# Scaling the first chunk's tokens behind the projection, spreading beta by a product, and a new order on all engines, in a one-core transformer block

## The chip, the core and the metric

The kernel runs on one core of one Trainium2 chip. The metric is the time of one execution on the device, in microseconds, taken as the median of several timed runs. Beside the timed runs there is one profiled execution with its own time; its trace records what each engine did: TensorE (PE, with its weight loads PEld), VectorE (DVE), ScalarE (ACT), GpSimd (POOL), SyncE (SP, which here issues transfers) and the DMA queues. Times within the trace count from its first instruction.

## The reference

One pre-layernorm block on 2048 tokens of width 576, all in bfloat16: an attention with a memory, and a feed-forward part.

```python
def _layernorm(x, axis=-1, eps=1e-05):
    m = jnp.mean(x, axis=axis, keepdims=True)
    v = jnp.var(x, axis=axis, keepdims=True)
    return (x - m) / jnp.sqrt(v + eps)

def _A_ref(x, wq, wk, wv, wo, beta):         # H = 32 heads of 18, N = 4 segments of L = 512 tokens
    q, k, v = x @ wq, x @ wk, x @ wv         # cut into heads and segments
    g = _sigmoid(beta).reshape(1, H, 1, 1)
    for s in range(N):
        p = softmax(q[s] @ k[s].T * 18 ** -0.5 + causal mask)
        a_dot = p @ v[s]
        a_mem = phi(q[s]) @ M / (phi(q[s]) @ z + 1e-06)
        o[s] = g * a_mem + (1.0 - g) * a_dot
        M, z = M + phi(k[s]).T @ v[s], z + phi(k[s]).sum(tokens)
    return o @ wo                            # phi(t) = t + 1 where t > 0, exp(t) elsewhere

def _B_ref(x, w1, b1, w2, b2):               # F = 4608
    return _gelu(x @ w1 + b1) @ w2 + b2

h = x + _A_ref(_layernorm(x), ...)
out = h + _B_ref(_layernorm(h), ...)
```

## The kernel before

The 2048 tokens are worked in 8 chunks of 256, each of two tiles of 128 tokens; two chunks make a segment. The work on TensorE is written as streams (Python generators) that are woven into each other:

- `stream_P(tl)`, one for each of a chunk's two tiles: load x, layernorm, transpose the normalised tile (on TensorE in the first two chunks, by a transposing DMA later), project it to q, k and v. A projection is five products (`mm5`, lines 607 to 610: four on 128 rows of the width, one on the last 64 with a row of zeros). In the first chunk it is cut into six groups of 288 columns, later into four of 432. Each group's bank of PSUM is evicted to bfloat16 by `move` (lines 687 to 689), a plain copy on ScalarE or VectorE.
- `stream_A`: scores of a query tile against key tiles (`scores`, line 817, four heads at once on 32 rows of the array each), one exponential over all four score banks (line 823, 128x2048), the causal mask on GpSimd or VectorE (lines 828 and 830), the weighted sum (line 849 or 862) and its division (`finish`). There is one set of score banks.
- `stream_M`: the memory matrices; `stream_B(tl)`: the product with wo, the residual, the second layernorm.
- `stream_F1` and `stream_F2`: the feed-forward part. F1 takes w1 in 9 column groups per chunk (`load_w1`, streamed again for every chunk into a ring of buffers), with products on 128 rows (line 1167) and on 64-row halves (line 1154), adds b1 in the eviction (line 1175 or 1177) and applies the gelu on ScalarE (line 1189). F2 (line 1223) multiplies by w2, which stays on the chip.

The **layernorm** (lines 612 to 635) is statistics on VectorE (line 617, two halves), their aggregation and the addition of epsilon (lines 621 and 622), a power of -0.5 on GpSimd (line 627), and then one VectorE instruction that subtracts the mean and multiplies by the power (line 631). For the first chunk all of it stands ahead of the first product.

**Beta** is loaded by a GpSimd DMA into all 128 partitions (line 571); `gates` makes the sigmoid and its complement of it on ScalarE and VectorE.

**What sets the order.** While the program is built, the function first simulates itself with a list of estimated durations and due times (`op`, `begin`, `step`, `SLACK`, `PHASES`); this makes a list of operations. What is sent to the engines is something else: `arranged` (line 1313) goes through the written list `ORDER` of operation numbers, found by a search, and issues each in that order; a negative number means that the operation runs on its second engine (VectorE in place of ScalarE, say). `PLACE` gives the PSUM bank of each use. Every engine runs its instructions strictly in this order and waits on semaphores where it must, so a late operation holds up all that stand behind it on its engine. That includes SP, which issues nearly all transfers from one queue, and may have eight under way. At the start, where TensorE has nothing to do, products of zeros are put in (line 1295).

The products use four shapes of the array: 128x128, 64x128 (line 1154), 32x128 (scores) and 128x32 (weighted sums of later chunks).

## Time and profile before

| | |
|---|---|
| timed runs | 461.86, 466.97, 467.87 us (median 466.97) |
| profiled execution | 460.12 us, of which the trace's span is 458.4 |
| granted TensorE clock | 1.00 |
| PE busy | 449.2 us, 98% of the span, 6078 products |
| ACT busy | 318.9 us, 70% |
| DVE busy | 291.9 us, 64% |
| POOL busy | 152.4 us, 33% |
| DMA | 83.40 MB, 182 GB/s on average |

A busy time is the union of an engine's instructions. Products are pipelined: one starts before the one ahead of it has ended, so the mean time of a product is longer than the step between two starts, and a short stall can hide in the busy time. "Idle before" in a row is what the engine waited for just ahead of this instruction, with the releaser that came last.

### The profile page before, as it was taken

To read this page: it belongs to the slowest core of one execution; us is meant where nothing else is said; L and a number is where in the kernel's file an instruction comes from. 1 tells how busy PE (TensorE), PEld (TensorE's weight loads), DVE (VectorE), ACT (ScalarE), POOL (GpSimd) and SP (SyncE) were. 2 spreads that over 40 slices of the span, in tenths; PEclk is the share of its full clock that TensorE was granted. 3 is DMA by queue.
4 is the path that set the end of the run, shared out by engine and by line. 5 is a ranking of instruction groups with operands and counts; after the bars stand their busy time and mean duration, and the time that the engine had idled before them with its cause. 6 is when DMAs were issued, how large, how long until landed. Compare 5 with 4: busy or idle time off the path is not lost.

```text
span 458.4 us, 14431 instructions
## 1 busy us (share of the span) xinstructions
PE 449.2 (98%) x6078; PEld 333.8 (73%) x6078; DVE 291.9 (64%) x765; ACT 318.9 (70%) x309; POOL 152.4 (33%) x208
## 2 busy tenths in 40 slices
PE   7999999999999999999999999999999999999997
PEld 5778676676777777666677777677777888888874
DVE  6888888777788667778774757686564535212311
ACT  5888889887987958896565986788757954260420
POOL 5667254482345025573241312521222101000000
PEclk9999999999999999999999999999999999999999
DMA  7998978798997679799878787568966867574001
GB/s 217 312 308 163 262 191 159 166 220 176 180 183 200 197 207 215 136 187 200 160 172 165 209 214 169 141 166 166 248 194 188 189 189 228 160 222 137 28 14 39
DMA packets 137521, 83.40 MB, mean 182 GB/s; under 512 B 72800, under 2 KB 135664, under 8 KB 137456
## 3 DMA queue, kind: packets, MB, share of 16 engines
q1 hardware_dynamic: 137424, 82.47, 73.8%
q8 instruction: 47, 0.77, 0.7%
q14 instruction: 18, 0.15, 0.1%
q0 software_dynamic: 32, 0.01, 0.0%
HBM read 59.44 MB, written 6.49 MB: 144 GB/s over the span
## 4 chain that ended last, share of the span: by engine, by line
PE 85%; DMA 6%; DVE 4%; ACT 1%; POOL 1%; SPq 1%; issue 1%; ACTq 0%; POOLq 0%; DVEq 0%
PE bank L1223 23%; PE bank L1167 18%; PE bank L609 11%; PE late L1223 6%; PE st L817 5%; PE late L1167 4%; PE ox L849 4%; PE bank L1154 3%; PE bank L610 3%; DMA o_col<-oT 2%; PE bank L1127 2%; DMA xT<-o_nat 1%; PE ox L1167 1%; DMA KT<-qk_pad 1%; DMA w1g<-in_B_w_dram 1%; ACT pt L823 1%
## 5 line engine op out<-in xcount | busy, mean ns | idle before, releaser
L823 ACT ACTIVATE pt<-st 128x2048 bf16<-128x2048 f32 x80 | 150.2, 1877 | 42.3 <-PE st L817 22.7
L1223 PE MATMUL bank<-w_sb,hT 128*128 128x288 bf16 (+1 forms) x900 | 132.2, 288 | 0.0
L1223 PEld LDWEIGHTS <-hT 128*128 128x128 bf16 x1152 | 109.1, 98 | 30.0 <-issue 1.5
L828 POOL TENSOR_SCALAR_AFFINE_SELECT pt<-pt 128x512 bf16<-128x512 bf16 x87 | 56.2, 661 | 99.8 <-ACT pt L823 99.7
L1167 PE MATMUL bank<-xn2T,w1g 128*128 128x256 bf16 x656 | 82.2, 273 | 0.3 <-DMA w1g<-in_B_w_dram 0.3
L1189 ACT ACTIVATE hT<-hT 128x1536 bf16<-128x1536 bf16 (+3 forms) x26 | 66.3, 2567 | 22.9 <-DVE hT L1177 22.8
L1167 PEld LDWEIGHTS <-w1g 128*128 128x128 bf16 x752 | 70.4, 98 | 15.8 <-issue 5.7
L1177 DVE TENSOR_TENSOR hT<-bank,b1T 128x512 bf16<-128x512 f32 x73 | 49.6, 687 | 47.0 <-PE bank L1167 46.8
L609 PE MATMUL bank<-wqkv,xT 128*128 128x432 bf16 (+1 forms) x268 | 57.2, 336 | 1.0 <-DVE hT L1177 0.5
L609 PEld LDWEIGHTS <-xT 128*128 128x128 bf16 x400 | 37.0, 97 | 21.6 <-issue 1.5
L1175 ACT ACTIVATE hT<-bank,b1T 128x256 bf16<-128x256 f32 x64 | 26.7, 474 | 23.9 <-PE bank L1167 23.4
L817 PE MATMUL st<-QT,KT 32*128 32x128 bf16 x1280 | 32.3, 217 | 0.4 <-DMA KT<-qk_pad 0.3
L1223 PE MATMUL late<-w_sb,hT 128*128 128x288 bf16 x216 | 32.2, 286 | 0.0
L1167 PEld LDWEIGHTS <-wqkv 128*128 128x128 bf16 x288 | 27.3, 98 | 5.2 <-issue 1.3
L817 PEld LDWEIGHTS <-KT 32*128 32x128 bf16 x1280 | 18.6, 92 | 16.2 <-issue 12.8
L1033 POOL TENSOR_TENSOR h_t<-h_t,b_bc 128x576 f32<-128x576 f32 x16 | 20.7, 1297 | 23.3 <-issue 16.6
L849 PE MATMUL ox<-pt,v_aug 128*32 128x128 bf16 x1184 | 25.9, 221 | 0.0
L830 DVE TENSOR_TENSOR pt<-pt,causal 128x512 bf16<-128x512 bf16 x41 | 19.4, 484 | 9.2 <-ACT pt L823 9.2
L849 PEld LDWEIGHTS <-v_aug 128*32 128x32 bf16 x1184 | 17.3, 96 | 7.6 <-issue 4.5
L610 PE MATMUL bank<-wqkv,xT 65*128 65x432 bf16 (+1 forms) x67 | 22.6, 338 | 0.0
L1227 DVE TENSOR_TENSOR ot<-bank,hc 128x288 bf16<-128x288 f32 x24 | 10.9, 456 | 16.8 <-PE bank L1223 10.5
L1177 DVE TENSOR_TENSOR hT<-late,b1T 128x512 bf16<-128x512 f32 x13 | 8.6, 686 | 19.6 <-PE late L1167 19.5
(148 smaller groups left out, 633.7 us busy)
## 6 DMA issues: line engine op xcount, KB each, us to landing
w1g<-in_B_w_dram SPq DMA_DIRECT2D x49, 512.0 KB, 4.7
wqkv<-in_B_w_dram SPq DMA_DIRECT2D x18, 512.0 KB, 4.8
w_sb<-in_B_w_dram SPq DMA_DIRECT2D x6, 864.0 KB, 8.2
hd<-h_t SPq DMA_DIRECT2D x14, 288.0 KB, 3.2
hc<-hd SPq DMA_DIRECT2D x28, 144.0 KB, 3.0
w1g<-in_B_w_dram SPq DMA_DIRECT2D x98, 32.0 KB, 3.2
x_b<-in_A_x_dram SPq DMA_DIRECT2D x18, 144.0 KB, 3.9
hT<-in_B_w_dram SPq DMA_DIRECT2D x5, 512.0 KB, 4.1
```

What stands on the lines that cost most here:

```text
L609: nc.tensor.matmul(out=out_ap, lhsT=lhsT_of(slice(0, P), k), rhs=rhs_of(slice(0, P), k), start=(k == 0), stop=False)
L610: nc.tensor.matmul(out=out_ap, lhsT=lhsT_of(slice(0, KTAIL), 4), rhs=rhs_of(slice(0, KTAIL), 4), start=False, stop=True)
L817: nc.tensor.matmul(out=st4[:, i, n * P:(n + 1) * P], lhsT=KTs[(c - c % 2 + kt // 2) % 3][rows, g, (kt % 2) * P:(kt % 2 + 1) * P], rhs=QTs[ ...
L823: op("ACT", 1.88, lambda: nc.scalar.activation(out=pt[:], in_=st4[:], func=ACT.Exp, scale=scale), sk, [("pt", slot, n) for n in range(4)], ...
L828: either(("POOL", 0.64, lambda part=part: nc.gpsimd.affine_select(out=part, in_=part, pattern=[[0, 4], [1, P]], compare_op=ALU.is_ge, fill ...
L849: nc.tensor.matmul(out=ox[32 * i:32 * i + 32, g % 4 * P:(g % 4 + 1) * P], lhsT=v_flat[(2 * s0 + kt) % 6][:, h * E:h * E + 32], rhs=pts[slo ...
L1033: op("POOL", 1.29, lambda: nc.gpsimd.tensor_tensor(out=h_t[:], in0=h_t[:], in1=b2_bc[:], op=ALU.add), ["b2"], [("h", tl)], slack=SLACK["hb"])
L1167: nc.tensor.matmul(out=bank(b)[:, a * Q:(a + 1) * Q], lhsT=w1_main(wt)[:, k, (2 * (h % 2) + a) * P:(2 * (h % 2) + a + 1) * P], rhs=xn2T[c ...
L1175: nc.scalar.activation(out=hT[:, f + a, :], in_=bank(b)[:, a * Q:(a + 1) * Q], func=ACT.Identity, bias=b1T[:, f + a:f + a + 1])
L1177: either(("DVE", 0.69, lambda hT=hT, f=f, b=b: nc.vector.tensor_tensor(out=hT[:, f:f + 2, :], in0=bank(b)[:].rearrange("p (a w) -> p a w", ...
L1189: op("ACT", (f1 - f0) * Q * 0.00083 + 0.18, lambda hT=hT, f0=f0, f1=f1: nc.scalar.activation(out=hT[:, f0:f1, :], in_=hT[:, f0:f1, :], fun ...
L1223: nc.tensor.matmul(out=acc, lhsT=hT[:, q, tl * P:(tl + 1) * P], rhs=w2_sb[:, q, hs], start=(q == 0), stop=(q == NF - 1))
```

## The change

It has these parts.

1. In the first chunk, `layernorm` with `late_scale` only subtracts the mean (VectorE), right behind the aggregation. The addition of epsilon and the power run on GpSimd and give a factor per token (`rstd0`), and the six evictions of each of the two tiles multiply by it in place of copying.
2. Beta is loaded into one partition by SP. A product of a row of ones with it spreads it over 128 partitions in a PSUM bank, and the exponential of `gates` reads it there. `gates` is now called by `stream_F1`.
3. The buffers of w1 in the last chunks are assigned by a fixed rule (`W1Q`), and from chunk 6 (`LATE`) F1 opens up to three groups at once, and the gelu runs in pieces of six blocks. Before, both came with the end of the attention.
4. Estimated durations in `finish` are other ones. These only steer the build.
5. `ORDER` and `PLACE` are new from the first entry to the last, so every engine's order is new. The first loads in SP's queue are, before: x tile 0, tail of wk, x tile 1, b1, wk, x tile 3, tail of wq, wq, a tail of w1, x tile 2, wv. After: x tile 0, x tile 1, wk, beta, tail of wk, x tile 2, tail of wq, wq, a tail of w1, x tile 3, tail of wv, x tile 5, wv. On GpSimd the factor of tile 1 is computed ahead of that of tile 0, with a memset of `b1_rows` between them.

```diff
     ORDER = [
...
     PLACE = (
...
-    LATER, AHEAD, NS, MOST = 0, 5, 1, 3
+    LATER, AHEAD, NS, MOST, LATE, W1Q = 0, 5, 1, 3, 6, 45
...
-    def gates():
-        op("ACT", 0.25, lambda: nc.scalar.activation(out=g_bc[:], in_=beta_bc[:], func=ACT.Exp, scale=-1.0), ["beta"], ["g"],
+    def gates(b):
+        op("PE", 0.06, lambda: nc.tensor.matmul(out=bank(b)[:, 0:H], lhsT=ones[0:1, :], rhs=beta_row[0:1, :], start=True, stop=True),
+           ["beta", "ones"], [b])
+        op("ACT", 0.25, lambda: nc.scalar.activation(out=g_bc[:], in_=bank(b)[:, 0:H], func=ACT.Exp, scale=-1.0), [b], ["g"],
...
-        o = op("POOL", 0.75, lambda: nc.gpsimd.dma_start(out=beta_bc[:], in_=A_beta.partition_broadcast(P)), (), ["beta"])
-        transfer(o, 1, 6.5, (), ["beta"]).apart = True
+        memset("DVE", 0.09, ones[0:1, :], 1.0, "ones")
+        memset("DVE", 0.06, mhalf[:], -0.5, "mhalf")
+        dma(9, lambda: nc.sync.dma_start(out=beta_row[0:1, :], in_=A_beta.rearrange("(o h) -> o h", o=1)), (), ["beta"])
...
-            layernorm(f"p{tl}", x_p[tl][:], ("x_p", tl), xn1[tl], ("xn1", tl), False, SLACK["ln0"] + 3 * tl)
+            layernorm(f"p{tl}", x_p[tl][:], ("x_p", tl), xn1[tl], ("xn1", tl), False, SLACK["ln0"] + 3 * tl, late_scale=True)
...
-    def layernorm(who, src, skey, dst, dkey, f32, slack):
+    def layernorm(who, src, skey, dst, dkey, f32, slack, late_scale=False):
...
+        if late_scale:
+            rstd = rstd0[who]
...
+        def apply():
+            for to, f0, f1 in ((0, 0, D), (D, 512, D))[0:2 if f32 else 1]:
+                if late_scale:
+                    nc.vector.tensor_scalar(out=dst[:, to:to + f1 - f0], in0=src[:, f0:f1], scalar1=mv[:, 0:1], scalar2=None, op0=ALU.subtract)
+                else:
+                    nc.vector.tensor_scalar(out=dst[:, to:to + f1 - f0], in0=src[:, f0:f1], scalar1=mv[:, 0:1], scalar2=rstd[:],
+                                            op0=ALU.subtract, op1=ALU.mult)
...
+        def plus(e):
+            e.tensor_scalar(out=rstd[:], in0=mv[:, 1:2], scalar1=EPS, scalar2=None, op0=ALU.add)
...
+            if not late_scale:
+                plus(nc.vector)
+
+        def power():
+            if late_scale:
+                plus(nc.gpsimd)
+            nc.gpsimd.tensor_tensor(out=rstd[:], in0=rstd[:], in1=mhalf[:], op=ALU.pow)
...
             def move(dst, src, n, key):
+                if c == 0:
+                    either(("ACT", n * 0.00083 + 0.16, lambda: nc.scalar.mul(out=dst, in_=src(), mul=rstd0[who][:])),
+                           ("DVE", n * 0.00104 + 0.16, lambda: nc.vector.tensor_scalar(out=dst, in0=src(), scalar1=rstd0[who][:], scalar2=None,
+                                                                                       op0=ALU.mult)), [b, "rs0" + who], [key])
+                    return
...
+        yield need(None, bank_slots, ["beta", "ones"])
+        b = bank_slots.take()
+        gates(b)
+        bank_slots.give(b)
...
-                while late and len(some) < MOST and fg + len(some) < NG and some[-1] + 1 in w1_at:
+                while c >= LATE and len(some) < MOST and fg + len(some) < NG:
                     some.append(some[-1] + 1)
...
-                    alone = NCH - 1 in done_A
+                    alone = c >= LATE
```

More of the change, by code (lines that the diff above doesn't have):

```diff
@@ L466 @@
     causal = sbuf("causal", [P])
-    mhalf = sbuf("mhalf", [1], F32)
     maskcol = sbuf("maskcol", [1], F32)
@@ L501 @@
           for k in ("p0", "p1", "b0", "b1")}
+    rstd0 = {k: sbuf(f"rstd0_{k}", [1], F32) for k in ("p0", "p1")}
+    mhalf = sbuf("mhalf", [1], F32)
     hd = tc.dram_tile([S, D], F32, name="hd")
@@ L564, in constants @@
         op("DVE", 0.27, lambda: nc.vector.memset(pq[:], 0.0), (), ["pq"])
-        memset("DVE", 0.06, mhalf[:], -0.5, "mhalf")
         for tl in range(2):
@@ L913, in finish @@
             to, key = (o_dst, ok) if c < 2 else (t1[:], ["t1"])
[L914 removed]
+            op("DVE", 0.40, lambda: nc.vector.tensor_tensor(out=to, in0=heads[:, :, 0:Dh], in1=r1b, op=ALU.mult), [Ck, "r1"], key, slack=slack, port=True)
             if c > 1:
@@ L1058, in w1_of, with more_w1 @@
         return w1_tiles[w1_at[n]], w1_at[n]
-    def more_w1(done):
-        w1_free.append(w1_at[done])
-        if ("w1q", 0) not in readers and not any(g in waits for g in projections) and max(o.end for o in readers["wqkv_pad"]) < now:
+    def more_w1(done=None):
+        if done is not None:
+            w1_free.append(w1_at[done])
+        if ("w1q", 0) not in readers and len(done_P) == NCH:
             w1_free.extend(("w1q", j) for j in range(3))
```

44 lines of the change are left out of this document (21 added, 23 removed), and 230 rows, old and new, of the table ORDER.

## The prediction

> **What bounds the kernel now.** I read the page first, for which engine has no room; then the busy time by stretches of the span, for where TensorE still has room (columns: stretch, length, busy time of PE, PEld, DVE, ACT, POOL with counts, granted clock, DMA share, GB/s); then TensorE's waits.
>
> ```profile
> span 458.4 us, 14431 instructions
> PE 449.2 (98%) x6078; PEld 333.8 (73%) x6078; DVE 291.9 (64%) x765; ACT 318.9 (70%) x309; POOL 152.4 (33%) x208
> ...
> 0.00:8.40 8.40, 5.31 (x39) 3.94 (x40) 5.06 (x24) 4.42 (x9) 5.12 (x13) 1.00 0.65 166
> 8.40:16.00 7.60, 7.60 (x92) 6.03 (x90) 5.68 (x21) 5.42 (x10) 3.20 (x5) 1.00 1.09 326
> ...
> 340.00:455.00 115.00, 115.00 (x1154) 91.25 (x1152) 37.92 (x81) 51.27 (x62) 8.22 (x10) 1.00 0.51 147
> 455.00:458.40 3.40, 0.13 (x1) 0.00 (x0) 0.61 (x1) 0.00 (x0) 0.00 (x0) 1.00 0.14 43
> ```
>
> TensorE is the bound, at a granted clock of 1.00 throughout. Of its 458.4 - 449.2 = 9.2 us of idle time, 8.40 - 5.31 = 3.1 lie before the first projection and 3.3 behind the last product; 2.8 us are left for everything between. So an order can win much only at the head, and has little to win, but all to lose, in the middle. The waits name the same places:
>
> ```profile
> PE bank L1295 <- DVE pq L564: 1.8, 1, 1.8
> PE bank L640 <- DVE xn L631: 1.2, 1, 1.2
> PE bank L609 <- DMA xT<-o_nat: 0.7, 1, 0.7
> ```
>
> The columns are the total, the number and the longest. Six waits of 0.5 us or less follow. The first two are the head; the rest is the 2.8 us. The part of the head that counts is also longer than its idle time, as TensorE is filled there with products of zeros (L1295). From the timeline of the head, and as last row from the chain of work that ended last (start, length: x landing):
>
> ```profile
> 0.79 0.40 SPq L529 DMA_DIRECT2D x_p<-in_A_x_dram  x1
> 1.25 0.56 SPq L533 DMA_DIRECT2D wqkv<-in_A_wk_dram  x1
> 1.86 0.57 SPq L529 DMA_DIRECT2D x_p<-in_A_x_dram  x1
> 3.17 0.38 SPq L1093 DMA_DIRECT2D b_rows<-in_B_b_dram  x1
> 3.60 0.41 SPq L532 DMA_DIRECT2D wqkv<-in_A_wk_dram  x1
> ...
> 3.00 0.84 DVE L617 BATCH_NORM_STATS2 stats_p<-x_p 128x6 f32<-128x288 bf16 x2 [0.53 <-DMA x_p<-in_A_x_dram]
> 3.87 0.21 DVE L621 BATCH_NORM_AGGREGATE mv_p<-stats_p 128x2 f32<-128x12 f32 x1
> 5.33 0.56 POOL L627 TENSOR_TENSOR rstd_p<-rstd_p,mhalf 128x1 f32<-128x1 f32 x1
> 6.08 0.42 DVE L631 TENSOR_SCALAR xn<-x_p,mv_p,rstd_p 128x576 bf16<-128x576 bf16 x1
> 6.24 0.67 POOL L627 TENSOR_TENSOR rstd_p<-rstd_p,mhalf 128x1 f32<-128x1 f32 x1 [0.35 <-DVE rstd_p L622]
> 6.56 0.45 PE L640 MATMUL bank<-ident,xn 128*128 128x128 bf16 x5 [1.20 <-DVE xn L631]
> 8.21 0.44 PE L640 MATMUL ox<-ident,xn 128*128 128x128 bf16 x5
> 8.49 0.65 PE L609 MATMUL bank<-wqkv,xT 128*128 128x288 bf16 x4
> ...
> 9.10 0.65 PE L609 MATMUL bank<-wqkv,xT 128*128 128x288 bf16 x4
> ...
> 8.69 0.69 ACT L675 COPY xT<-ox 128x640 bf16<-128x640 bf16 x1 [3.47 <-PE ox L640]
> ...
> 1.86 3.02 DMA x_p<-in_A_x_dram
> ```
>
> The mean of tile 0 is known at 3.87 + 0.21 = 4.08, but its tokens are normalised only from 6.08: the power on GpSimd comes between, behind a long memset there. The second tile lands at 4.88, since its load stands third in the queue. The first projection starts at 8.49.
>
> **The change part by part.**
>
> *Late scaling and the reordered head.* Tile 0 no longer waits for the power: subtraction 0.04 us behind the mean, 4.12 + 0.42 = 4.54, transposes (0.45) to 5.0, ScalarE's copy (0.69) to 5.75. Tile 1's load is now second in the queue, so it leaves near 1.25 and lands 3.02 later, 4.3; statistics 0.84 behind tile 0's subtraction to 5.4, mean 5.65, subtraction 6.1, transposes 6.15. In TensorE's new order they and one filler stand ahead of the first projection, which gives 6.15 + 0.28 + 0.1 = 6.55, against 8.49: **-1.9 us**. For this the key weights must be there; their main part stood fifth, behind a load of b1 that waited for a memset (issued 3.17), and is now third (about 1.8), and the 64-row tail fifth (about 2.8):
>
> ```profile
> wqkv<-in_A_wk_dram SPq DMA_DIRECT2D x1, 576.0 KB, 3.9
> wqkv<-in_A_wv_dram SPq DMA_DIRECT2D x1, 576.0 KB, 6.3
> ...
> wqkv<-in_A_wk_dram SPq DMA_DIRECT2D x1, 72.0 KB, 3.4
> ...
> 6.94 0.43 SPq L532 DMA_DIRECT2D wqkv<-in_A_wv_dram  x1
> ```
>
> (DMA issues: KB each, us to landing; last row from the timeline.) The key weights land at 1.8 + 3.9 = 5.7 and 2.8 + 3.4 = 6.2: in time.
>
> *What is late next: the power.* The evictions of the first chunk now multiply by it. GpSimd's new order computes tile 1's first: add and power behind 5.65, then a memset of 128x128 (0.21), then tile 0's. The add on 128x1 has no row. Its ends are nothing and the power itself (0.56). Nearest are two rows of one kind and two widths: 0.66 at 512 columns and 0.29 at 128 give 0.17 at one; I take 0.2.
>
> ```profile
> L828 POOL TENSOR_SCALAR_AFFINE_SELECT pt<-pt 128x512 bf16<-128x512 bf16 x87 | 56.2, 661 | 99.8 <-ACT pt L823 99.7
> 11.04 0.29 POOL L574 TENSOR_SCALAR_AFFINE_SELECT causal<-causal 128x128 bf16<-128x128 bf16 x1
> 9.30 0.46 DVE L689 CAST qk_pad<-bank 128x288 bf16<-128x288 f32 x1 [1.38 <-PE bank L610]
> ```
>
> Tile 0's factor: 5.7 + 0.2 + 0.6 + 0.2 + 0.2 + 0.6 = 7.5; the eviction (0.46) ends at 8.0. Groups of projections follow each other by 9.10 - 8.49 = 0.61, so the fourth starts at 8.4 and is the first that needs this bank: 0.4 to spare, or 0.3 late if the add costs 0.56. Scaled evictions cost ScalarE the price of an activation with an operand, 474 ns at 256 columns, so some 0.50 at 288 against 0.40 for the plain copy: ten of them, 1 us of an engine with room at this place.
>
> ```profile
> L1175 ACT ACTIVATE hT<-bank,b1T 128x256 bf16<-128x256 f32 x64 | 26.7, 474 | 23.9 <-PE bank L1167 23.4 <-DVE hT L1177 0.2
> L688 ACT CAST qk_pad<-bank 128x288 bf16<-128x288 f32 x10 | 4.0, 400 | 4.3 <-PE bank L610 4.1 <-DVE v_aug L689 0.2
> ```
>
> *And the value weights.* They landed at 6.94 + 6.3 = 13.2 with 2.55 MB queued up to and including them; now it is 2.76 MB, since reloads of x go ahead. The queue fills 1.8 us sooner (3.60 to 1.8) and the extra 0.21 MB cost 0.65 at the 326 GB/s of the 8.40:16.00 row: 12.1. Their first product stands 5.8 us of TensorE work behind the first projection (eight groups of 0.61 and two sets of eight transposes, 0.055 each by rows below): 12.4. Margin 0.3; a loss of 0 to 0.8. For this and the power together I take 0.35 back. From the first projection on, TensorE's work is 0.15 us longer (below). **Head: -1.9 + 0.35 + 0.15 = -1.4**, bounds -1.9 and 0.
>
> *Beta by a product.* GpSimd loses a broadcast load, SP gains a load of 64 bytes, fourth in its queue (one issue, 0.5 us, counted above), TensorE one small product; the exponential then frees its bank at about 6.0, ahead of the first projection, which takes that bank. Nothing, or 0.3 us if the tiny load needs 4 us.
>
> *The order from 14 us on.* TensorE's instructions are the same but for 24 fillers in place of 29, plus beta: 6074 products against 6078. What an order changes is how often the array's tile shape switches: 277 times before, 280 after, counted in the two programs. A switch costs 0.1 us:
>
> ```profile
> 8.15 0.22 PE L1096 MATMUL bank<-ident,b_rows 128*128 128x128 bf16 x1
> ...
> 34.84 0.44 PE L640 MATMUL bank<-ident,o_nat 128*128 128x128 bf16 x5
> 35.22 0.40 PE L817 MATMUL st<-QT,KT 32*128 32x128 bf16 x16
> ...
> 30.73 1.88 ACT L823 ACTIVATE pt<-st 128x2048 bf16<-128x2048 f32 x1 [0.17 <-PE st L817]
> 33.19 1.88 ACT L823 ACTIVATE pt<-st 128x2048 bf16<-128x2048 f32 x1 [0.17 <-PE st L817]
> ```
>
> Five transposes in 0.44, one in 0.22, so a step of 0.055; a sixth would start at 34.84 + 0.28 = 35.12, the scores start at 35.22. Two of the three lie around beta's product, ahead of the first projection; behind it stands one more, and b1's product (0.06) has moved there too: the +0.1 to 0.2 counted above. [...]
>
> The same rows show the loop that can stall the middle: one set of score banks, so exponentials follow each other at 33.19 - 30.73 = 2.46 at best. With each product at the step its shape shows, the gaps between score groups hold less than 2.46 us of TensorE work five times before (0.47 us short in all) and seven times after (0.57); less than 2.6 us 13 and 20 times. The last score group has 337 us of work ahead of it before, 314 after: attention is packed tighter and the plain FFN tail is longer, where the 340.00:455.00 row shows TensorE without a gap. ScalarE gets 12 table loads instead of 18. I price tighter packing less relief at **+0.4**, bounds -2.7 (all middle waits gone) and +4.
>
> ```profile
> L1189 ACT ACT_TABLE_LOAD x9 | 11.5, 1283 | 0.5 <-DVE hT L1177 0.4
> ```
>
> By this row six loads less are 7.7 us of ScalarE. [...]
>
> **Sum.** -1.4 + 0.4 = -1.0 on the profiled execution's 460.12 us (its span 458.4 and 1.7 around it): 459.1. The timed runs lie above it, 461.86, 466.97 and 467.87; the same step from their median gives **466.0**. Two per cent (9 us) is about what a measurement of this kernel can tell from no change, and more than the 3.1 + 2.8 us of idle time before the tail.
>
> **Rivals.**
> 1. *ScalarE becomes the bound in the packed attention; slower than before.* For: twelve score groups in the last 29 us of attention work, 2.3 to 2.8 us apart; twelve exponentials of 1.88 are 22.6, and some 6 us of other ScalarE work falls there, so it is full. Against: the head of the present kernel runs as tight and loses 0.1 to 0.2 a time. Price: 0.2 us at each of the 20 gaps below 2.6 is 4, less the 1.4 of the head: 469.5. It decides where waits on L823 in the middle sum to over 1.4 us.
> 2. *The change doesn't do what it says:* the wait for the power only moves to the first evictions, or the wait for x to the value weights, and the start of the scores stays where it was. For: GpSimd computes tile 1's factor first, and the margins are 0.4 and 0.3. Against: the chain to the first projection holds no power any more, which took 4.08 to 6.08 of the old one; one of the two margins would have to fail by some 1.9 us. Head 0: 460.5, from the median 467.4.
> 3. *The new order also removes the middle waits:* -1.4 - 2.7: 462.9. For: each is a lone wait for a bank or a transfer. Against: the new order has as many short distances as the old.
>
> **How the numbers follow.** Forecast 0.45, first rival 0.22, second 0.15, third 0.13, else 0.05 (a late weight in the FFN, or a level of the runs that has nothing to do with the change). The cases span 462.9 to 469.5; the timed runs of one kernel alone spread from -5 to +1 around their median, which stretches it to 458.5 to 471. Over 2% faster (below 457.6) needs the third and the lowest level together: 0.06. Over 2% slower (above 476.3) needs the first at more than double its price: 0.07.
>
> **What would show it.** First projection near 6.6 instead of 8.5; the first scaled eviction near 7.6 with GpSimd's power just ahead of it; no wait for the value weights over 0.8; TensorE's waits after 14 us summing to 2 to 4 us with L823 among them; the last exponential some 23 us sooner; ScalarE 8 us less of table loads. Wrong would be a first projection after 7.5, or waits in the middle of over 6 us.

## The result, and the profile after

Six timed runs of the changed kernel have a median of **458.33 us** (457.49 to 459.63), six of the kernel before 465.17 (461.86 to 467.87). The ratio is **0.986, with an interval of 0.981 to 0.991**: faster, by less than the 2% that counts here as a difference, and by 6.8 us where the prediction had 1.0. The profiled execution took 458.34 us, as long as the median; that of the kernel before, with 460.12, is shorter than each of its six timed runs. So the two traces differ by 1.8 us only, and two questions are to be kept apart: what these 1.8 us are, and where the timed runs of the kernel before lose some 5 us that its trace doesn't show.

From the page of the changed kernel:

```profile
span 456.6 us, 14417 instructions
PE 448.5 (98%) x6074; PEld 333.2 (73%) x6074; DVE 286.9 (63%) x761; ACT 315.3 (69%) x316; POOL 147.4 (32%) x202
```

The busy time by stretches, of the kernel before (the same execution as above, cut otherwise) and then of the changed one; the columns are the stretch, its length, the busy time of PE, PEld, DVE, ACT and POOL, the granted clock, the DMA share and GB/s:

```profile
0.00:14.50 14.50, 11.41 (x96) 8.72 (x96) 9.74 (x42) 8.61 (x18) 8.32 (x18) 1.00 0.83 230
14.50:340.00 325.50, 322.66 (x4831) 233.86 (x4831) 243.61 (x643) 259.05 (x231) 135.84 (x180) 1.00 0.83 194
340.00:455.00 115.00, 115.00 (x1154) 91.25 (x1152) 37.92 (x81) 51.27 (x62) 8.22 (x10) 1.00 0.51 147
455.00:458.40 3.40, 0.13 (x1) 0.00 (x0) 0.61 (x1) 0.00 (x0) 0.00 (x0) 1.00 0.14 43
```

```profile
0.00:14.50 14.50, 12.18 (x99) 9.20 (x100) 10.75 (x39) 9.16 (x19) 8.12 (x19) 1.00 0.83 245
14.50:340.00 325.50, 322.46 (x4974) 232.73 (x4972) 246.66 (x666) 262.22 (x236) 135.67 (x180) 1.00 0.87 194
340.00:453.90 113.90, 113.89 (x1008) 91.30 (x1005) 29.13 (x57) 43.94 (x62) 3.62 (x4) 1.00 0.52 145
453.90:456.60 2.70, 0.00 (x0) 0.00 (x0) 0.31 (x1) 0.00 (x0) 0.00 (x0) 0.95 0.18 55
```

TensorE's idle time is length less busy time: in the head 3.09 and then 2.32 us, from 14.5 to 340 us 2.84 and 3.04, behind the last product 3.27 and 2.70 (the last piece that VectorE evicts is now 144 columns, 0.31 us, in place of 432, 0.61). From 340 us on it is 0.00 and 0.01. Its busy time fell by 0.67, of which the five products of zeros fewer are 0.2 (4.93 and 4.73 us in the head). The sum is -0.77 + 0.20 + 0.01 - 0.57 - 0.67 = -1.8 us, the difference of the spans.

The head, from the timeline of the changed kernel and, as last row, the first scores of the kernel before:

```profile
4.75 0.74 PE L657 MATMUL ox<-ident,xn 128*128 128x128 bf16 x5
5.29 1.50 PE L1326 MATMUL bank<-pq 128*128 128x256 bf16 x10
7.00 0.17 PE L550 MATMUL bank<-beta_row,ones 1*128 1x32 bf16 x1 [0.21 <-DMA beta_row<-in_A_beta_dram]
7.50 0.65 PE L612 MATMUL bank<-wqkv,xT 128*128 128x288 bf16 x4
10.22 0.36 PEld L612 LDWEIGHTS <-xT 128*128 128x128 bf16 x4 [0.41 <-DMA wqkv<-in_A_wq_dram]
14.77 0.40 PE L841 MATMUL st<-QT,KT 32*128 32x128 bf16 x16
```

```profile
14.53 0.40 PE L817 MATMUL st<-QT,KT 32*128 32x128 bf16 x16
```

The first projection is a full microsecond earlier (7.50 in place of 8.49), and the first scores are 0.24 us later. Two things lie between. The wait for the query weights costs TensorE 0.27 us (the group that needs them starts 0.88 behind the one before it in place of 0.61). And more work now stands ahead of the scores, 1.0 us of it: the first group with the value weights (0.61) and the transposes of a third tile (0.40), which come behind the scores in the kernel before. So the start of the scores undercounts the head: by the work done, my estimate is a gain of 0.61 + 0.40 - 0.24 = 0.8 us here, and 0.5 and 0.6 in two more traces of the changed kernel, where the scores start at 15.01 and 14.94. Between the transposes of the two tiles stand ten products of zeros, and behind them beta's product waits for its load. The loads of the weights (KB each, us to landing) of the changed kernel:

```profile
wqkv<-in_A_wk_dram SPq DMA_DIRECT2D x1, 576.0 KB, 5.5
wqkv<-in_A_wq_dram SPq DMA_DIRECT2D x1, 576.0 KB, 5.8
wqkv<-in_A_wv_dram SPq DMA_DIRECT2D x1, 576.0 KB, 4.7
```

They were issued at 1.71, 4.36 and 8.42, so they landed at 7.2, 10.2 and 13.1; the kernel before had 7.5, about 10.7 (SP's wait for it ends by 10.81) and 13.2. So the key weights came 0.3 us earlier and the value weights 0.1. The value weights are now the thirteenth load in place of the eleventh, and they were issued 1.5 us later, since SP had to wait for 1.1 us before the eleventh, their tail:

```profile
7.28 0.47 SPq L535 DMA_DIRECT2D wqkv<-in_A_wv_dram  x1
```

It left only when the third load, the key weights, had landed (7.2), and the sixteenth left at 10.20, when the eighth, the query weights, had. In the kernel before SP waits for the eighth ahead of the sixteenth, which left at 10.81, and for the eleventh ahead of the nineteenth, which left at 13.22 (1.0 us each): in all four places a load left when the one eight places ahead of it was there.

TensorE's waits in the changed kernel:

```profile
PE ox L1326 <- DVE maskcol L539: 2.0, 1, 2.0
PE bank L1185 <- DMA w1g<-in_B_w_dram: 0.9, 1, 0.9
PE bank L612 <- DMA xT<-xn: 0.8, 1, 0.8
PE st L841 <- issue: 0.5, 1, 0.5
PE bank L1198 <- DMA hT<-in_B_w_dram: 0.4, 1, 0.4
```

Behind the head they sum to 3.1 us with 0.3 and 0.2 of two more. All but two name transfers; the two (0.5 ahead of scores, 0.2) have no releaser in the trace. No row names the exponential.

### The profile page after: what moved, and what is told of

Read it like the earlier page. It is cut to its first block, busy times and chain, and to the rows that moved or that the text cites. A ratio compares the mean times of both kernels' runs of the same rounds, so it can differ in the third digit from the quotient of the medians.

```text
span 456.6 us, 14417 instructions
## 1 busy us (share of the span) xinstructions
PE 448.5 (98%) x6074; PEld 333.2 (73%) x6074; DVE 286.9 (63%) x761; ACT 315.3 (69%) x316; POOL 147.4 (32%) x202
## 4 chain that ended last, share of the span: by engine, by line
PE 89%; DMA 5%; SPq 3%; ACT 1%; DVE 1%; issue 1%; ACTq 0%
PE bank L1254 21%; PE bank L1198 17%; PE bank L612 13%; PE late L1254 6%; PE late L1198 6%; PE st L841 5%; PE ox L873 4%; PE bank L613 3%; PE bank L1185 3%; PE bank L1158 2%; PE ox L1254 1%; PE ox L1198 1%; SPq L367 1%; DMA hT<-in_B_w_dram 1%; DMA w1g<-in_B_w_dram 1%; DMA beta_row<-in_A_beta_dram 1%
## 5 line engine op out<-in xcount | busy, mean ns | idle before, releaser
L1254 PE MATMUL bank<-w_sb,hT 128*128 128x288 bf16 x864 | 126.3, 286 | 0.0
L1198 PE MATMUL bank<-xn2T,w1g 128*128 128x256 bf16 x656 | 85.3, 273 | 0.0
L852 POOL TENSOR_SCALAR_AFFINE_SELECT pt<-pt 128x512 bf16<-128x512 bf16 x81 | 52.4, 658 | 95.2 <-ACT pt L847 88.8
L1208 DVE TENSOR_TENSOR hT<-bank,b1T 128x512 bf16<-128x512 f32 x70 | 47.3, 685 | 41.5 <-PE bank L1198 41.1
L1206 ACT ACTIVATE hT<-late,b1T 128x256 bf16<-128x256 f32 x32 | 13.3, 477 | 38.7 <-PE late L1198 22.3
L1206 ACT ACTIVATE hT<-bank,b1T 128x256 bf16<-128x256 f32 x56 | 23.5, 473 | 20.1 <-PE bank L1198 20.1
L1254 PE MATMUL late<-w_sb,hT 128*128 128x288 bf16 (+1 forms) x216 | 33.9, 296 | 0.0
L1198 PEld LDWEIGHTS <-wqkv 128*128 128x128 bf16 x272 | 26.0, 98 | 4.6 <-issue 0.8
L854 DVE TENSOR_TENSOR pt<-pt,causal 128x512 bf16<-128x512 bf16 x47 | 22.4, 479 | 8.3 <-ACT pt L847 8.1
L646 POOL TENSOR_TENSOR rstd_b<-rstd_b,mhalf 128x1 f32<-128x1 f32 x16 | 9.3, 582 | 56.2 <-DVE rstd_b L636 53.8
```

The lines of the kernel that those rows point to most:

```text
L852: either(("POOL", 0.64, lambda part=part: nc.gpsimd.affine_select(out=part, in_=part, pattern=[[0, 4], [1, P]], compare_op=ALU.is_ge, fill ...
L854: ("DVE", 0.42, lambda part=part: nc.vector.tensor_tensor(out=part, in0=part, in1=causal[:].unsqueeze(1).to_broadcast([P, 4, P]), op=ALU.m ...
L1198: nc.tensor.matmul(out=bank(b)[:, a * Q:(a + 1) * Q], lhsT=w1_main(wt)[:, k, (2 * (h % 2) + a) * P:(2 * (h % 2) + a + 1) * P], rhs=xn2T[c ...
L1206: nc.scalar.activation(out=hT[:, f + a, :], in_=bank(b)[:, a * Q:(a + 1) * Q], func=ACT.Identity, bias=b1T[:, f + a:f + a + 1])
L1208: either(("DVE", 0.69, lambda hT=hT, f=f, b=b: nc.vector.tensor_tensor(out=hT[:, f:f + 2, :], in0=bank(b)[:].rearrange("p (a w) -> p a w", ...
L1254: nc.tensor.matmul(out=acc, lhsT=hT[:, q, tl * P:(tl + 1) * P], rhs=w2_sb[:, q, hs], start=(q == 0), stop=(q == NF - 1))
```

## The experiments

Two theories stood against each other on the 5 us that the trace of the kernel before lacks. **A**: single transfers land late, an engine that reads them waits at the head of its queue, and TensorE waits for what stands behind; how late differs from run to run, and the new order has fewer such places. **B**: chance. On the head there were three: late scaling carries it, beta's row does, or the weights do.

### The changed kernel again, twice

No edit.

> The changed kernel once more, beside the kernel before. Theory A (the kernel before loses some 5 us in its runs at a place which its profiled execution did not show, and the new order does not have that place): again near 458.3 with a spread under 2 us, while the kernel before again spreads over 462 to 468. Theory B (chance of the chip or the day): the two come within 3 us of each other, or the changed kernel spreads as widely.

> The changed kernel once more on this chip, as the measure for the two runs ahead of it: 457.5 to 460.8.

Measured: 459.51 us (458.78 to 460.75, 4 runs) beside 466.01 (461.85 to 471.07, 13 runs) of the kernel before, ratio 0.987 (0.980 to 0.995); then 457.58 (456.94 to 458.72, 6 runs) beside 463.98 (459.91 to 468.17, 23 runs), ratio 0.988 (0.985 to 0.991). The gain holds, and so does the difference in spread. It isn't chance.

### Scaling ahead of the projection again, in the new order

```diff
     ORDER = [
...
-            56, 29, 3, 31, 54, 2, 32, 89, 70, 33, 90, 71, 64, 72, 34, 74, 36, 9, 35, 75
+            56, 29, 30, 3, 54, 2, 32, 70, 33, 71, 64, 72, 34, 35, 31, 89, 90, 74, 36, 9, 75
...
-                if late_scale:
+                if False:
...
-            if not late_scale:
+            if True:
                 plus(nc.vector)
...
-            if late_scale:
+            if False:
                 plus(nc.gpsimd)
...
-                    either(("ACT", n * 0.00083 + 0.16, lambda: nc.scalar.mul(out=dst, in_=src(), mul=rstd0[who][:])),
...
+                    either(("ACT", n * 0.00083 + 0.16, lambda: nc.scalar.copy(out=dst, in_=src())),
+                           ("DVE", n * 0.00104 + 0.16, lambda: nc.vector.tensor_copy(out=dst,
...
```

(30 and 35 are the powers of the two tiles, 31 is the first subtraction, 89 and 90 are the transposes of tile 0 and their copy.)

> The new order with the scaling put back ahead of the projection: the power on GpSimd stands before each tile's subtraction again, the evictions of the first chunk copy, all else is the changed kernel. Theory 'late scaling carries the head' (the prediction's): first projection near 8.3 in place of 7.5, total 0.8 to 1.4 above the changed kernel, 459.1 to 459.7. Theory 'other things hold the head' (beta's row lands at 7.0 and the query weights at 10.2 whatever the first tile does): first projection 7.5 to 8.0, the wait for the query weights shrinks by what the first projection loses, total within 0.4 of the changed kernel. Theory 'late scaling is behind the 7 us between the medians': 463 or more.

Measured: 459.24 us (457.92 to 460.73), against 459.51 in the same company. The first projection came at 8.02 and the first scores at 14.93, where that run of the changed kernel had 7.63 and 15.01. The work ahead of the scores is the same in both. **Late scaling is worth nothing that can be seen**: its 0.4 us at the first projection are gone at the scores.

### Beta's load second in the queue

```diff
     ORDER = [
-            13, 0, 20, 16, 17, 1
+            13, 0, 22, 20, 16, 17, 1
...
-            48, 18, 81, 22, 52, 84
+            48, 18, 81, 52, 84
```

> The changed kernel with beta's load of 64 bytes moved from fourth to second in the queue of loads. Beta's product then need not wait until 7.0. Theory 'beta's row holds the head': first projection 6.7 to 7.0, total 0.5 to 0.8 less, 457.5 to 457.8. Theory 'the weights hold the head': first projection 6.7 to 7.0 as well, but the wait for the query weights at 10.2 grows from 0.4 to about 1.0, total within 0.3 of the changed kernel.

Measured: 459.45 us (457.71 to 460.94). Beta's product started at 6.83 in place of 7.11, the first projection at 7.35 in place of 7.63, and the scores at 14.83 in place of 15.01. In neither of these two traces does the product wait for its load; it waits for the ten products of zeros ahead of it, which took 1.61 us here and 1.89 there, so the 0.28 can't be put down to the load. The query weights are again waited for (0.3 us at 10.3, not the 1.0 that was expected). The total is unchanged, as "the weights hold the head" says; a run further below (the queue mended) shows that this isn't the whole of it.

### Late scaling alone, in the order before

```diff
-            layernorm(f"p{tl}", x_p[tl][:], ("x_p", tl), xn1[tl], ("xn1", tl), False, SLACK["ln0"] + 3 * tl)
+            layernorm(f"p{tl}", x_p[tl][:], ("x_p", tl), xn1[tl], ("xn1", tl), False, SLACK["ln0"] + 3 * tl, late_scale=True)
```

with the rest of `layernorm` and `move` as in the changed kernel; `ORDER` and beta as before.

> The kernel before, in its own order, with the late scaling alone: tile 0 and 1 only centred, the add on GpSimd, scaled evictions. Theory 'late scaling by itself is worth the head': first projection at 7.4 or earlier against 8.49, total 1 us less than the kernel before. Theory 'only together with the order' (the second tile's load stands third, the key weights' tail lands at 7.0): first projection 7.8 to 8.4, total within 0.5 of the kernel before. Theory A says that the wide spread of 462 to 468 stays, since its place is in the order behind the head; if instead the runs fall to 458 to 460 with a small spread, the place is in the head.

Measured: 465.53 us (461.67 to 468.93), ratio 0.999 (0.995 to 1.003); first projection at 8.57. The change to the arithmetic is worth nothing by itself, and the spread stays. The profiled execution was a long one (467.47 us), and so it shows what the trace of the kernel before hides. TensorE's waits; then VectorE and GpSimd in the timeline; then the busy time by stretches (line numbers are up to 20 higher here, the instructions are those of the kernel before):

```profile
PE bank L1147 <- ACT v_aug L708: 3.0, 1, 3.0
PE ox L869 <- DVE pt L850: 1.8, 1, 1.8
```

```profile
57.00 0.25 DVE L928 RECIPROCAL r<-o_col 128x16 f32<-128x16 bf16 x1 [2.32 <-DMA o_col<-oT]
57.62 0.49 DVE L929 TENSOR_TENSOR r<-r,omg_bc 128x16 f32<-128x16 f32 x1
58.14 1.15 DVE L816 TENSOR_SCALAR MZ_blk<-MZacc,maskcol 32x8 bf16<-32x8 f32 x1
60.33 0.97 DVE L709 CAST qk_pad<-bank 128x288 bf16<-128x288 f32 x2
```

```profile
57.33 0.76 POOL L848 TENSOR_SCALAR_AFFINE_SELECT pt<-pt 128x512 bf16<-128x512 bf16 x1 [3.40 <-DVE r L928]
58.06 1.20 POOL L776 TENSOR_TENSOR phik_pad<-ek,phik_pad 128x576 bf16<-128x576 bf16 x1
```

```profile
56.00:62.17 6.17, 3.16 (x48) 2.15 (x47) 4.97 (x11) 2.60 (x3) 1.93 (x2) 1.00 0.76 192
62.17:65.58 3.41, 3.41 (x68) 2.85 (x65) 2.43 (x8) 1.50 (x3) 2.73 (x4) 0.50 0.50 90
65.58:69.00 3.42, 3.42 (x56) 2.55 (x53) 2.05 (x4) 3.09 (x3) 0.87 (x2) 1.00 0.65 206
```

The same place in the kernel before's own trace:

```profile
55.01 0.25 DVE L908 RECIPROCAL r<-o_col 128x16 f32<-128x16 bf16 x1 [0.70 <-DMA o_col<-oT]
55.63 0.17 DVE L909 TENSOR_TENSOR r<-r,omg_bc 128x16 f32<-128x16 f32 x1
55.83 0.23 DVE L796 TENSOR_SCALAR MZ_blk<-MZacc,maskcol 32x8 bf16<-32x8 f32 x1
57.10 0.46 DVE L689 CAST qk_pad<-bank 128x288 bf16<-128x288 f32 x1
57.93 0.38 PE L1127 MATMUL bank<-xn2T,w1g 128*128 128x128 bf16 x4 [0.16 <-ACT v_aug L688]
```

Read it from the first row: the transfer of `o_col`, issued at 51.14 (50.76 before), is there at 57.0 (55.0), and VectorE stands for 2.32 us (0.70). Now its next instructions meet two of GpSimd's: the small product takes 0.49 in place of 0.17, ending at 58.11 where GpSimd's ends at 58.09, the next 1.15 in place of 0.23, ending at 59.29 where GpSimd's ends at 59.26. So the projections are evicted 3.2 us later (0.4 of it because the transfer was issued that much later), and TensorE stands for 3.0 us in place of 0.16. And then the clock: for 3.41 us TensorE is granted half of it, which costs 1.7 us more (my estimate, 0.5 x 3.41). One transfer that lands 1.6 us later relative to its issue makes some 4.5 us: 1.6 of lateness, 1.2 beside GpSimd's two instructions, and 1.7 of clock. At 362 us a late load of `hc` does the same with 1.8, and there TensorE's products keep their step: four of 256 columns take 0.44 us from 363.00 on, as they do in the kernel before's trace at 362.42.

### The kernel before once more

No edit.

> The kernel before once more, for a second trace of it. Theory A (transfers that land late hold up VectorE at the head of its queue, and through it TensorE): single stalls of TensorE of 1 to 3 us, at 61 us behind the reader of o_col on VectorE, at 362 us behind the reader of hc, or at other readers of transfers, that together make up the time above 460. Theory C (TensorE itself is slower in such runs, by its clock): no stall over 1 us, the same products take longer, a granted clock under 1.

Measured: 461.96 us. The same place, with the reader of QT behind that of `o_col`:

```profile
PE bank L1127 <- ACT v_aug L688: 2.4, 1, 2.4
```

```profile
55.65 0.25 DVE L908 RECIPROCAL r<-o_col 128x16 f32<-128x16 bf16 x1 [1.34 <-DMA o_col<-oT]
58.17 0.84 DVE L875 TENSOR_SCALAR pq<-QT 128x512 bf16<-128x512 bf16 x1 [0.97 <-DMA QT<-qk_pad]
```

A stall of 2.4 us, no lost clock. Theory C (TensorE slower by itself) falls for these two traces: one has a stall and keeps the clock, the other loses it behind a stall.

### The two loads of w2 apart, and a load of hc ahead of one of w1

```diff
     ORDER = [
...
-            421, 382, 398, 245, 387, 399, 388, 339, 367, 351
+            421, 382, 398, 387, 399, 388, 339, 367, 351
```

and 245 stands between 284 and 257, at 35.5 us. In the second kernel also:

```diff
-            2223, 2126, 2212, 2204, 2245
+            2223, 2204, 2126, 2212, 2245
```

> The kernel before with one thing moved: of the two loads of w2 (864 KB each) that stand side by side in the queue at 45.8 and 46.3 us, ahead of the transposing transfers of o_col and QT, the first goes out at 34 us instead. Theory A: o_col lands at 55 to 55.5 in every run, the stall of TensorE at 61 us (3.2 us in the trace of the late scaling alone) is gone, the median is 1.5 to 3 us below the kernel before. Theory 'many small places': within 1 us of the kernel before.

> As the run before, and the 144 KB load of hc at 348 us stands ahead of the 512 KB load of w1 in place of behind it. Theory A: the stall at 362 us (2.0 us in the trace of the late scaling alone) is gone as well, the median is 3 to 5 us below the kernel before, near 461 to 463. Theory 'many small places': within 1.5 us of the kernel before.

Measured: 461.11 us (458.86 to 463.06) and 460.57 (459.21 to 463.07), beside 464.08 of the kernel before; ratios 0.995 (0.991 to 0.999) and 0.994 (0.990 to 0.997). **One load moved by 10 us in the queue brings 3 us**, as theory A has it. It does so by making the stall that costs the clock rare: 9 of the 19 runs of the kernel before in this company lost clock, one of these 20. Among the runs that kept it the medians are only 0.8 us apart (461.5 and 460.7). In the first trace `o_col` is there before VectorE asks for it:

```profile
54.25 0.24 DVE L908 RECIPROCAL r<-o_col 128x16 f32<-128x16 bf16 x1
```

TensorE's idle time from 45 to 115 us is 0.24 us there (69.76 busy of 70). The second load moved, of `hc`, added 0.5 us at most, within the intervals. The trace of the second kernel has the stall once more (2.0 us, behind QT) and others beside it: the place became rarer, it didn't go.

### A third load of w2 beside the two

```diff
     ORDER = [
...
-            224, 204, -268, 345, 219, 179
+            224, 204, -268, 219, 179
...
-            399, 388, 339, 367, 351, 389
+            399, 388, 339, 367, 345, 351, 389
```

> The kernel before with the suspected cost made larger: a third load of w2 (864 KB, issued at 22.9 us) moved beside the other two at 46 us, so that 2.6 MB stand ahead of the transfers of o_col and QT in place of 1.7. Theory A (late transfers at the head of VectorE's queue): QT lands 2.5 to 3 us later, the stall of TensorE near 58 us is 4 to 6 us in place of 0.3 to 3.2; such a stall also costs the full clock for some microseconds, as in the trace of the late scaling alone; median 4 to 6 us above the kernel before. Theory 'many small places': within 1.5 us of it.

Measured: 466.80 us (464.80 to 470.18, 10 runs), ratio 1.007 (1.004 to 1.011), 2.8 us above the kernel before. TensorE's wait, VectorE's wait and the stretch behind them:

```profile
PE bank L1127 <- ACT v_aug L688: 4.7, 1, 4.7
```

```profile
DVE r L908 <- DMA o_col<-oT: 7.2, 5, 5.3
```

```profile
62.39:65.80 3.41, 2.97 (x29) 2.97 (x29) 3.16 (x10) 2.63 (x3) 1.35 (x3) 0.50 0.65 125
```

The stall is as long as was expected, and all ten runs lost clock (mean 0.991 to 0.996). The loss against the kernel before is smaller than the 4 to 6 us expected, probably because that has part of this stall in many runs itself. The same lever, both ways: for the kernel before, the place of these loads is shown as a cause of some 3 us.

### The pair of loads put into the changed kernel

```diff
     ORDER = [
...
-            276, 306, 297, 365, 298
+            276, 306, 297, 298
...
-            395, 575, 477, 409, 513
+            395, 575, 477, 365, 271, 409, 513
```

(271 was some fifteen entries ahead of this place.)

> The changed kernel with the suspected cause put in: its loads of w2 at 33.2 and 43.7 us are put side by side behind QT's transfer, at about 46 us, as the kernel before has them. If what the new order gains is the place of these loads in the queue: o_col and KT land 2 us later, a stall of 1 to 3 us between 53 and 62 us, median 461 to 463. If the new order instead leaves more work between a transfer and its reader: no stall over 0.5 us there, median within 1 us of the changed kernel.

Measured: 458.62 us (457.66 to 460.83, 5 runs), where the changed kernel had 457.58 in the same company. The profiled run has the stall, with the loss of clock behind it; the other four runs kept the clock:

```profile
PE bank L1158 <- DVE hT L1164: 1.8, 1, 1.8
```

```profile
61.89:65.30 3.41, 3.41 (x68) 3.02 (x61) 1.97 (x5) 2.40 (x2) 1.47 (x2) 0.50 1.05 242
```

Neither expectation is met: not 461 to 463, but lost clock in one run of five. So what the new order gains isn't only the place of these two loads: put back side by side, they cost it 1.0 us, where taking them apart brought the kernel before 3. That it leaves more work between such a transfer and TensorE is argued, not shown. In the changed kernel's first trace VectorE waits for `o_col` 3 times, 1.0 us in all; in the kernel before:

```profile
DVE r L908 <- DMA o_col<-oT: 3.9, 6, 1.1
```

But this sum doesn't tell the kernels apart: the second trace of the kernel before has 2.7 us in 5 waits, two more of the changed kernel 3.0 in 6 and 1.8 in 3.

### The queue of the changed kernel mended, in two ways

First with beta second, x tiles 2, 3 and 5 and a tail of w1 behind the value weights, and three loads further on put ahead of their neighbours:

```diff
     ORDER = [
-            13, 0, 20, 16, 17, 1
+            13, 0, 22, 20, 16, 17, 1
...
-            147, 83, 6, -106, 113
+            147, 83, 6, 355, 8, 64, 9, -106, 113
...
-            536, 495, 489, 389, 539, 497, 597, 532, 598
+            536, 495, 489, 532, 389, 539, 497, 597, 598
...
-            1402, 1332, 1519, 1413, 1520
+            1402, 1332, 1519, 1271, 1413, 1520
...
-            1583, 1475, 1568, 1615, 1584
+            1583, 1475, 1568, 1616, 1615, 1584
```

> The changed kernel with its queue of loads mended where its traces show TensorE waiting: beta's row second, the query and value weights ahead of 460 KB that are read later, and at 72, 211 and 232 us the one load that TensorE waits for put ahead of one or two others. Theory 'the weights hold the head': query weights land near 9.2 in place of 10.2 to 10.4, value weights near 12 in place of 13.1 to 13.5, scores start 0.4 to 1.0 us earlier; the waits at 77, 216 and 239 us, 0.5 to 1.5 each, lose half; median 1 to 2.5 us below the changed kernel. Theory 'TensorE's own work holds the head': the weights land earlier but the scores do not start earlier, within 0.7 us of the changed kernel.

Measured: 462.47 us (459.95 to 464.46), **4.9 us worse** than the changed kernel. The query weights landed at 9.7 (issued at 3.72, 5.9 to landing), and their projection still started only at 10.17, without a wait: TensorE's own queue holds it, with the ten products of zeros, which took until 7.2:

```profile
5.29 1.97 PE L1326 MATMUL bank<-pq 128*128 128x256 bf16 x10
17.17 0.69 PE L657 MATMUL bank<-ident,xn 128*128 128x128 bf16 x5 [2.64 <-DVE QT L758]
```

```profile
DVE stats_p L622 <- DMA x_b<-in_A_x_dram: 3.2, 1, 3.2
```

```profile
16.98:20.39 3.41, 3.22 (x35) 2.38 (x35) 2.60 (x9) 2.00 (x2) 1.27 (x3) 0.50 0.86 258
```

The tiles of x that were "read later" are read by VectorE's statistics, ahead of an eviction that the next transposes need: 3.2 us of VectorE, 2.6 of TensorE, and the clock for 3.41 us; ten of the twelve runs lost clock. That is theory A's mechanism, made by hand. Then with the head left alone:

```diff
     ORDER = [
...
-            536, 495, 489, 389, 539, 497, 597, 532, 598
+            536, 495, 489, 532, 389, 539, 497, 597, 598
...
-            1403, 1376, 1517, 1531
+            1403, 1376, 1271, 1517, 1531
...
-            1583, 1475, 1568, 1615, 1584
+            1583, 1475, 1568, 1616, 1615, 1584
```

> The changed kernel with three neighbours swapped in the queue of loads and the head left as it is: at 71, 211 and 234 us the load that TensorE is seen waiting for goes ahead of the one or two before it (a store of hd, 32 KB of w1, 512 KB of w1 and a transposing transfer). Theory A (what counts is which transfer stands ahead of the one that is read next): the steps of 0.5 to 1.4 us at 77 us and of 1.0 to 1.7 at 239 us fall below 0.4, the step at 216 us by half; median 1 to 2.5 us below the changed kernel's 457.6 to 459.5, a ratio to the kernel before of 0.982 to 0.986. If the waits only move to what was put behind: 457.5 to 459.5, a ratio of 0.986 to 0.989, and new waits of TensorE beside those places.

Measured: 457.72 us (456.02 to 459.43, 6 runs), ratio 0.988 (0.983 to 0.992), the changed kernel's own. The stall at 239 us (0.9 in the first trace) is gone, those at 77 and 216 (0.4 and 0.8) are 0.4 and 0.3; others have come, at 79, 102 and 324 us:

```profile
PE bank L612 <- DMA xT<-o_nat: 1.3, 1, 1.3
PE bank L1185 <- DMA w1g<-in_B_w_dram: 1.0, 2, 0.8
PE bank L612 <- DMA xT<-xn: 0.9, 2, 0.6
```

The waits moved to what was put behind. No version tried beats the changed kernel beyond the noise.

### All runs of the kernel before, by granted clock

Beside these experiments the kernel before ran 66 times, and each run lists its mean granted clock. One stretch of 3.41 us at half clock is 1 - 0.5 x 3.41 / 465 = 0.996 of the mean.

| | runs | median | range |
|---|---|---|---|
| before, mean clock 0.998 to 1.000 | 36 | 462.3 us | 458.7 to 466.5 |
| before, 0.995 or 0.996 | 26 | 465.5 us | 463.2 to 468.4 |
| before, 0.993 | 4 | 467.6 us | 466.3 to 471.1 |
| w2 apart, and with hc | 20, one below 0.998 | 460.8 us | 458.9 to 463.1 |
| changed kernel | 16, none below 0.998 | 458.3 us | 456.9 to 460.8 |

So 30 of 66 runs of the kernel before lost clock; in each of the four traces, of any kernel here, that show such a stretch, a stall of TensorE stands at it. Of the difference of the first two rows, 3.2 us, one such stretch is 1.7; that the other 1.5 are longer stalls is not shown. The clock isn't the larger part of the gain: the runs of the kernel before that kept it still lie 4.0 us above the changed kernel. TensorE's idle time between 45 and 115 us, by the stretch view of each trace:

| trace | idle in 45 to 115 us | profiled time |
|---|---|---|
| before | 1.3 us | 460.1 |
| before again | 3.3 | 462.0 |
| late scaling alone | 3.6, and the clock | 467.5 |
| three loads of w2 | 5.4, and the clock | 466.8 |
| w2 apart | 0.2 | 459.3 |
| w2 apart, and hc | 4.2 | 462.3 |
| changed, three traces | 0.9, 1.2, 0.6 | 458.3, 459.1, 457.2 |
| changed, without late scaling; beta second; three swaps | 2.0, 1.2, 1.8 | 460.7, 460.9, 459.4 |
| changed, with the pair of w2 | 1.8, and the clock | 460.8 |
| changed, queue mended (its stall is at 14.5) | 1.7 | 463.1 |

## Why the prediction was right, and where its steps failed

That the kernel stays within 2% was right, in part by luck: the reason given, only 5.9 us of idle time ahead of the tail, came from one short execution, and the measured gain of 6.8 us is larger than that. The time was not right: 458.3 is 7.7 us below the 466.0 and just under the lower end of the range (of the 7.7, 1.8 are the median of three runs, 466.97, where six have 465.17). That lower end isn't what the prediction's own terms give, 462.9 - 5 = 457.9. And by its own sign of being wrong, a first projection after 7.5, the head failed: it came at 7.50, 7.63 and 7.86 in three traces.

1. **"The same step from their median gives 466.0."** This is the step that failed by most. It took the profiled execution as the kernel in its usual course, and the 5 us by which the timed runs lie above it as a level that stays. Some 3 of them are stalls which that execution happened not to have, and which no run of the changed kernel shows at a length that costs clock. The trace of before had a sign: six waits of VectorE for `o_col`, 3.9 us in all, on the reciprocal of `finish` (the row above). The sign is no proof, as the changed kernel has traces with nearly as much and no stall. The prediction read TensorE's waits alone, where the same thing showed as 0.16 us.
2. **"For this the key weights must be there ... land at 5.7 and 6.2: in time", and "they and one filler stand ahead of the first projection".** Both failed. The first projection came at 7.50, not at 6.55. The key weights took 5.5 us, not the 3.9 of the row, and landed at 7.2; that it is the transfers under way beside them is likely, but not shown. The tokens were ready as forecast (tile 1's subtraction ends at 5.94, forecast 6.1). But ten products of zeros that stand between the transposes of the two tiles were left out of the sum. They start 0.21 us apart at first and 0.11 later, the change comes at another time in each trace, and the ten took 1.50 to 2.12 us in five traces, so they end between 6.8 and 7.4.
3. **Beta: "nothing, or 0.3 us if the tiny load needs 4 us".** It needed 4.8 and made TensorE wait for 0.21 in the first trace, not at all in two others. The term was of the right size, and with the load second in the queue the total is the same.
4. **"12.1 ... margin 0.3" for the value weights.** They landed at 13.1, as they were issued at 8.42: the sum let the queue fill 1.8 us sooner, but it stood from 6.13 to 7.28 for the key weights to land. No wait came of it, since the first group that needs them started at 13.75, not at 12.4. The power was in time (7.11 + 0.57 = 7.68 for tile 0, predicted 7.5, first scaled eviction at 8.40), the two additions took 0.31 and 0.22 us, estimated at 0.2.
5. **"Head: -1.4".** The scores start 0.24 us later, not 1.4 earlier; with the 1.0 us of work counted that was put ahead of them, the head gained 0.5 to 0.8 us, about half. TensorE's idle time in the head fell by 0.77, but the kernel before, executed once more, had 2.31 us there, without any change: that figure hangs on how long the products of zeros take, which fill the rest.
6. **"+0.4" for the middle** was right for the profiled executions: +0.20, with waits of 3.1 us where 2 to 4 were named. That the exponential would be among them was wrong, nearly all are transfers. The tail's 0.57 and the 0.67 of busy time weren't in the sum.
7. **The rivals.** ScalarE didn't become the bound: table loads fell as worked out (18 to 12), the last exponential starts at 327.6 us in place of 351.8, and no wait names it. "The wait only moves" came true by the letter, the scores don't start earlier, though not by its two margins: the gain was halved by TensorE's own products of zeros and by the wait for the query weights. "The new order also removes the middle waits" had the right sign, but counted only the 2.8 us of this one execution.

Settled by runs of their own: late scaling brings nothing, in either order, and in the kernel before some 3 us are the transfers of `o_col` and QT behind two large loads. The new order keeps these loads apart, but the pair put back into it cost only one run of five its clock, so how it avoids the stall is not settled. That the gain comes from the order at all, and not from beta's product, from the fixed buffers of w1 or from opening groups earlier (parts 2 and 3 of the change), follows only by exclusion: the place of beta's load is worth nothing, but beta's product and part 3 were undone in no run. Not settled either: the 3.0 to 3.5 us that still lie between the kernel before with its loads apart (461.1 and 460.6) and the changed one (457.6 in a later company on the same chip). The first traces of the two kernels show 1.8 us of difference that is none of these stalls: 0.77 in the head, 0.57 in the tail and 0.67 of TensorE's busy time, less 0.20 in the middle. For the rest no run here names a place.

## What to carry to other kernels

A profiled execution that is shorter than all timed runs is a lucky one: ask what the runs have that it lacks before a difference is taken from it. Read the waits of the other engines for transfers as closely as those of the bound engine, since a wait of VectorE of 0.7 us, which cost TensorE 0.16 in one trace, was 2.32 in another, with 3.0 of TensorE behind it; whether a wait grows like this, only another trace or a run with the transfer moved can tell. A large load that nobody needs for 30 us (w2's, issued at 46 us, with the first product that reads w2 at 81) doesn't belong ahead of a small one that is read in 4 (`o_col`): one such load moved brought 3 us. And a wait that is mended by moving a neighbour back can make that neighbour late, as the tiles of x were, with 2.6 us of TensorE: ask who reads it.

## What the runs showed of the hardware

- **Four stalls came with a loss of clock, others didn't.** At TensorE's waits of 1.8 (the pair of w2), 2.6 (queue mended), 3.0 (late scaling alone) and 4.7 us (three loads of w2) the granted clock was 0.50 for 3.41 us each time. In the last three it began 0.2 us before the wait's end, 1.0 behind it and 0.4 before it. At waits of 2.4 us (the kernel before once more) and 2.0 (w2 apart, and hc) it stayed at 1.00, and behind another of 1.8 (late scaling alone, 362 us) the products kept their step of 0.11 us. So the length of the wait alone doesn't decide; what does is not shown.
- **Three small VectorE instructions ended together with GpSimd's.** In the trace of late scaling alone the one on 32x8 elements took 1.15 us, where it took 0.23 with GpSimd idle; GpSimd's addition, of 1.20 us, had started 0.08 us ahead of it, and both ended within 0.03 us of each other. The product on 128x16 ended within 0.03 us of GpSimd's too, at 57.62 us with 0.49 and at 360.31 with 1.21 in place of 0.17; the second time GpSimd's addition had started 0.09 us ahead. But at 57.29 us another instruction ran its usual 0.30 beside GpSimd's mask. What makes the three longer is not shown.
- **64 bytes can take 4.8 us.** Issued fourth, behind 0.9 MB, beta's load landed after 4.8 us in the first trace. The transfer of `o_col`, issued at 50.8 to 51.1 us in three traces of one order, was there 4.2, 4.9 and 5.9 us later; with one large load less ahead of it, in time (3.5 us at most), and with one more, 8.8 us later.
